# First chunk of a block-sparse attention with an expert MLP: exponentials in the gate's buffers, one head's ahead of the copies of the transposes

## The chip, the cores and the metric

The kernel runs on one core of a Trainium2 chip. The metric is the device time of one execution in microseconds (us). The engines are PE (matrix multiply), DVE (vector), ACT (scalar), POOL and SP; each takes its own instructions in the order in which the program wrote them, and they meet through semaphores. Transfers are issued from SP, ACT and POOL.

## What is computed

The attention is block sparse with 24 blocks of 32 positions. A query block sees itself and its neighbours, the first and last block, and three sampled blocks; the first and last query block see all. The attention's output goes through an MLP with the gate `h * sigmoid(1.702 h)`.

```python
scores = scale * np.matmul(q, k.transpose(0, 1, 3, 2))      # q, k, v: 4 x 8 heads x 768 x 64
scores = np.where(mask, scores, -1e9)
attn = np.exp(scores - scores.max(-1)); attn /= attn.sum(-1) + 1e-9
x = (attn @ v).transpose(0, 2, 1, 3).reshape(3072, 512)
h = x @ w_in                                                 # 512 x 2048
out = (h / (1 + np.exp(-1.702 * h))) @ w_out                 # 2048 x 512
```

## The kernel before

**Units and chunks.** A unit is 64 query rows (two blocks) of one batch, all eight heads; 48 units make six chunks of 512 tokens. The MLP works on one chunk at a time, in 16 steps over the hidden size, while the attention of the next chunk is spread between its matmuls (`tick`, `plan`). Only the attention of the first chunk has nothing to lie beside: `first` (L658) does items 0 to 8 (eight units of chunk 0 and one of chunk 1) before the first matmul of the MLP. All nine are sparse units.

**A round.** `first` is software pipelined. Its loop (L671) is called a round here, and round n works on three units:

- `scores` of unit n (L244): 32 small matmuls on PE into two banks (L260), one for each head of a pair. `least` (L278) adds the mask and takes the row minimum on DVE (L283, four instructions, two for each head), into `nm`. `exps` (L286) is four exponentials on ACT (L290), two for each head, which also sum the rows.
- `transposes` of unit n-1 (L296): eight on PE (L306), then two copies out of the banks on ACT into `pt` (L310), then the factors 1/sum on DVE (L360, L361). `values` of unit n-1 (L315): 64 small matmuls on PE (L331) that read `pt`; `normalise` (L365) scales their result into `x` on DVE (L373).
- `turn` of unit n-2 (L379): two transposes on PE (L384), a copy on ACT (`xhi`, L391), a subtraction on DVE (`xlo`, L392).

`self.early` is true in `first` alone. There `scores` hands back two steps, the minima of both heads and then the exponentials of both; `first` runs the second behind the copies of the transposes (L681). So ACT's round is: copy of `xhi`, two copies `pt`, four exponentials.

**Weights.** Between these steps `weights` (L398) converts the MLP's weights, read as pairs of 32-bit words of 64-bit floats: a load from ACT's queue into `raw` (L414, three buffers), an absolute value on ACT (L422), integer steps on DVE (L446, L452, L456), a copy on ACT (L459), a subtraction on DVE (L427). For the second matrix the result is saved to DRAM from ACT's queue (`ws`, L433), and `a` has three buffers, so that a later L422 waits until such a save has landed. From round 2 on, four steps of it run in each round: two between the minima and `turn` (L677), so that L422 stands on ACT ahead of `xhi`, and two at the end of the round (L686), with L456, L459 and the next load.

**Loads.** `loads` (L220) fetches keys and values for a pair of units into rings of two, from SP's and POOL's queues, once the pair before in the same slot has gone through its scores (keys) or its values.

**Buffers.** `ex` has four buffers of 384 columns (L289): the exponentials of unit n go over those of unit n-1, which the transposes have read by then. `ghi` and `glo` (L510, L518) are the split output of the gate, two buffers each of 512 columns; the MLP uses them from its first step on, and nothing before.

Of the kernel before, what the change touches and what calls it, by code (L numbers as in the profile page):

```python
# [9 lines left out]
F32 = mybir.dt.float32  # L10
F32R = mybir.dt.float32r
# [7 lines left out]
P = 128  # L19
# [12 lines left out]
CT = CU * UT  # L32
# [11 lines left out]
class Kernel:  # L44
# [57 lines left out]
    def indices(self):  # L102
# [7 lines left out]
        def take(shape):  # L110
            n = 1
            for k in shape:
# [8 lines left out]

        vblk = take([NB])
        first, second = slice(1, NB - 2, 2), slice(2, NB - 1, 2)
        nc.gpsimd.iota(vblk[3 * BLK:P, first], pattern=[[2, NU]], base=0, channel_multiplier=0,
                       allow_small_or_imprecise_dtypes=True)
# [20 lines left out]
        for i in range(NR):  # L146
            for cols, rows in ((first, slice(BLK * i, BLK * (i + 1))), (second, slice(BLK * (i + 1), BLK * (i + 2)))):
                nc.vector.tensor_copy(out=vblk[rows, cols], in_=sbw[rows, cols, i])
# [95 lines left out]
    def scores(self, g):  # L244
        nc, un, sparse = self.nc, g["unit"], self.sparse(g)
        r = g["k"]["n"] % RING
        g["k"]["scores"] -= 1
        if g["first"]:
            un["rs"] = self.small.tile([P, 2, NPAIR], F32, name="rs")
            un["nm"] = self.small.tile([P, 2, NPAIR], F32, name="nm")  # L250
        sps = self.psum("s", g["n"])
        if sparse:
            bi, n = un["b"] % 2, 2 * P
            kg = self.kg[r][:, :, bi].rearrange("p n (a s) -> p n a s", a=NPAIR)
            for i in range(2):
                for a in range(2):
                    for j in range(2):
                        for h in range(2):
                            pair, rows, c = 2 * i + a, slice(D * h, D * (h + 1)), 2 * a + j
                            nc.tensor.matmul(  # L260
                                sps[h][BLK * c:BLK * (c + 1), n * i:n * (i + 1)].rearrange("p (n s) -> p n s", s=BLK),
                                self.qt[r][rows, bi, UT * pair + BLK * j:UT * pair + BLK * (j + 1)],
                                kg[rows, 4 * j:4 * j + 8, pair], start=True, stop=True, tile_position=(D * h, BLK * c))
            parts = [(i, 0) for i in range(2)]
            bias = self.bias[:, un["u"]].rearrange("p (n o) -> p n o", o=1).broadcast_to([P, 8, BLK])
        else:
            kt = self.kg[r].rearrange("p n b c -> p (n b c)").rearrange("p (a s) -> p a s", a=NPAIR)
            i, half, n = g["i"], g["half"], S // 2
            for a in range(2):
                for h in range(2):  # L270
                    pair, rows = 2 * i + a, slice(D * h, D * (h + 1))
                    nc.tensor.matmul(sps[h][UT * a:UT * (a + 1), 0:n], self.qt[r][rows, 0, UT * pair:UT * (pair + 1)],  # L272
                                     kt[rows, pair, n * half:n * (half + 1)], start=True, stop=True, tile_position=(D * h, UT * a))
            parts = [(i, half)]
            bias = self.zero.broadcast_to([P, n])
        g["ex"] = {}

        def least(h):  # L278
            for k, (i, half) in enumerate(parts):
                at = sps[h][:, n * k:n * (k + 1)]  # L280
                if sparse:
                    at = at.rearrange("p (n s) -> p n s", s=BLK)
                nc.vector.tensor_tensor_reduce(out=at, in0=at, in1=bias, scale=-SCALE, scalar=3.0e38, op0=ALU.add, op1=ALU.min,  # L283
                                               accum_out=un["nm"][:, half, 2 * i + h:2 * i + h + 1])

        def exps(h):  # L286
            for k, (i, half) in enumerate(parts):
                c = 2 * i + h
                ex = g["ex"][h, k] = self.work.tile([P, 384], F32, name="ex", bufs=4)[:, 0:n]  # L289
                nc.scalar.activation(out=ex, in_=sps[h][:, n * k:n * (k + 1)], func=AF.Exp, bias=un["nm"][:, half, c:c + 1],  # L290
                                     scale=-1.0, accum_out=un["rs"][:, half, c:c + 1])

        return [lambda h=h: (least(h), exps(h)) for h in range(2)] if not self.early else [
            lambda: [least(h) for h in range(2)], lambda: [exps(h) for h in range(2)]]

    def transposes(self, g):  # L296

# [100 lines left out]
    def weights(self):  # L398
# [38 lines left out]
        fetch(1)  # L437
        yield
        first(0)
        for k, (f, i) in enumerate(todo):  # L440
            while i == 1 and f - WRING > self.downs - 1:
# [216 lines left out]
    def first(self):  # L658

        items = self.items[:CU + 1]  # L660
        assert items[CU]["unit"]["n"] == CU

        def finish(todo):
            while todo:
                todo.pop(0)()

        def weights(k):
            for _ in range(k):
                next(self.conv)

        for n, g in enumerate(items):  # L671
            if n == 1:
                next(self.conv)
            exps = self.scores(g)
            exps.pop(0)()
            if n > 1:
                weights(2)  # L677
                finish(self.turn(items[n - 2]))
            if n > 0:
                finish(self.transposes(items[n - 1]))  # L680
            finish(exps)  # L681
            if n > 0:
                finish(self.values(items[n - 1]))
            self.loads()
            if n > 1:
                weights(2)  # L686
        finish(self.turn(items[CU - 1]))
        self.loads()
# [64 lines left out]
```

## Time and profile before

| what | us |
|---|---|
| median of 3 runs (785.08 to 786.23) | 785.84 |
| the profiled execution, its own time | 782.75 |
| its span, first to last instruction | 781.1 |
| PE busy in the span | 738.6 (95%) |
| DVE busy | 412.8 (53%) |
| ACT busy | 383.5 (49%) |
| first matmul of the MLP starts at | 74.67 |

The profiled execution lies 3.09 us under the median of the runs. Times in rows are counted from the start of the span. A row of a timeline gives its start, its length, engine, line, operation, what it writes and reads, and in brackets how long the engine had been idle and what released it. A row that holds several instructions (x2) runs from the first's start to the last's end.

### The profile page before, as it was taken

To read this page: it belongs to the slowest core of one execution; us is meant where nothing else is said; L and a number is where in the kernel's file an instruction comes from. 1 tells how busy PE (TensorE), PEld (TensorE's weight loads), DVE (VectorE), ACT (ScalarE), POOL (GpSimd) and SP (SyncE) were. 2 spreads that over 40 slices of the span, in tenths; PEclk is the share of its full clock that TensorE was granted. 3 is DMA by queue.
4 is the path that set the end of the run, shared out by engine and by line. 5 is a ranking of instruction groups with operands and counts; after the bars stand their busy time and mean duration, and the time that the engine had idled before them with its cause. 6 is when DMAs were issued, how large, how long until landed. Compare 5 with 4: busy or idle time off the path is not lost.

```text
span 781.1 us, 19264 instructions
## 1 busy us (share of the span) xinstructions
PE 738.6 (95%) x7584; PEld 571.7 (73%) x7584; DVE 412.8 (53%) x1076; ACT 383.5 (49%) x950; POOL 57.1 (7%) x85
## 2 busy tenths in 40 slices
PE   2667999999999999999999999999999999999996
PEld 1445787767777777787877877877777777888884
DVE  3387779887644354445445544444554444443332
ACT  1567667666545444444444544444545454333332
POOL 5122001101000001000000000000000000000000
PEclk9699999999999999999999999999999999999998
DMA  8998887786644437664534465435574321041112
GB/s 267 281 367 296 251 254 256 251 259 222 206 162 153 117 114 219 173 177 129 161 117 145 142 175 156 137 115 163 161 229 153 93 98 42 28 108 40 55 41 55
DMA packets 61117, 128.22 MB, mean 164 GB/s; under 512 B 7569, under 2 KB 26514, under 8 KB 60514
## 3 DMA queue, kind: packets, MB, share of 16 engines
q1 hardware_dynamic: 46882, 80.50, 33.9%
q0 software_dynamic: 7232, 25.51, 10.1%
q10 hardware_dynamic: 6912, 20.97, 8.1%
q8 instruction: 60, 0.98, 0.5%
q14 instruction: 31, 0.25, 0.1%
HBM read 116.47 MB, written 10.49 MB: 163 GB/s over the span
## 4 chain that ended last, share of the span: by engine, by line
PE 78%; DMA 7%; DVE 7%; ACT 4%; issue 2%; SPq 1%; ACTq 0%; DVEq 0%
PE bank L491 11%; PE bank L541 10%; PE bank L542 10%; PE bank L537 10%; PE bank L493 10%; PE bank L492 10%; PE bank L260 5%; PE bank L306 4%; PE bank L331 4%; DMA ws<-a 3%; DMA kg<-in_kb_dram 2%; PE bank L339 2%; PE bank L272 2%; DMA raw<-in_moe_w_in_dram 2%; DVE a L452 1%
## 5 line engine op out<-in xcount | busy, mean ns | idle before, releaser
L491 PE MATMUL bank<-xhi,win 128*128 128x512 f32 x384 | 158.4, 412 | 1.2 <-ACT xhi L391 0.9
L290 ACT ACTIVATE ex<-bank,nm 128x256 f32<-128x256 f32 (+1 forms) x208 | 99.7, 492 | 115.4 <-DVE nm L283 113.6
L506 DVE SCALAR_TENSOR_TENSOR g<-g,bank 128x512 f32<-128x512 f32 x83 | 57.1, 687 | 183.8 <-ACT g L499 183.8
L541 PE MATMUL bank<-wout,ghi 128*128 128x512 f32 x384 | 154.1, 401 | 0.0
L542 PE MATMUL bank<-wout,ghi 128*128 128x512 f32 x384 | 151.7, 395 | 0.0
L493 PE MATMUL bank<-xhi,win 128*128 128x512 f32 x384 | 151.0, 393 | 0.0
L492 PE MATMUL bank<-xlo,win 128*128 128x512 f32 x384 | 150.0, 391 | 0.0
L499 ACT ACTIVATE g<-bank 128x512 f32<-128x512 f32 x96 | 57.5, 599 | 146.4 <-PE bank L493 146.1
L537 PE MATMUL bank<-wout,glo 128*128 128x512 f32 x384 | 107.7, 394 | 0.0
L480 DVE TENSOR_TENSOR wout<-wst,wout 128x512 fp32r<-128x512 f32 x80 | 55.4, 693 | 79.7 <-ACT wout L479 78.7
L511 ACT CAST ghi<-g 128x512 fp32r<-128x512 f32 x96 | 59.7, 622 | 54.6 <-DVE g L506 54.6
L491 PEld LDWEIGHTS bank<-xhi,win 128*128 128x128 f32 x384 | 72.1, 188 | 18.7 <-ACT xhi L391 1.1
L537 PEld LDWEIGHTS bank<-wout,glo 128*128 128x128 f32 x384 | 72.4, 189 | 17.3
L493 PEld LDWEIGHTS bank<-xhi,win 128*128 128x128 f32 x384 | 72.1, 188 | 16.3
L283 DVE CUSTOM_DVE_ANT_1 bank<-bank,bias 128x256 f32<-128x256 f32 x176 | 73.8, 440 | 19.3 <-PE bank L260 16.2
L542 PEld LDWEIGHTS bank<-wout,ghi 128*128 128x128 f32 x384 | 72.5, 189 | 15.6
L541 PEld LDWEIGHTS bank<-wout,ghi 128*128 128x128 f32 x384 | 72.2, 188 | 16.0
L492 PEld LDWEIGHTS bank<-xlo,win 128*128 128x128 f32 x384 | 72.3, 188 | 13.3 <-DVE xlo L392 0.3
L216 POOL DMA_INDIRECT vown<-in_v_dram,vidx x44 | 43.7, 994 | 496.9 <-PE bank L331 385.5
L260 PE MATMUL bank<-kg,qt 64*32 64x256 f32 x1408 | 55.8, 416 | 17.6 <-DMA vmid<-in_v_dram 10.5
L310 ACT COPY pt<-bank 128x512 f32<-128x512 f32 (+1 forms) x120 | 61.1, 563 | 19.4 <-PE bank L306 19.3
L331 PEld LDWEIGHTS bank<-vown,pt 128*32 128x32 f32 x1408 | 43.8, 113 | 31.8 <-ACT pt L310 16.0
(75 smaller groups left out, 821.8 us busy)
## 6 DMA issues: line engine op xcount, KB each, us to landing
wst<-ws SPq DMA_DIRECT2D x80, 256.0 KB, 2.7
kg<-in_kb_dram SPq DMA_DIRECT2D x136, 128.0 KB, 3.2
kg<-in_kb_dram SPq DMA_DIRECT2D x22, 384.0 KB, 4.9
raw<-in_moe_w_in_dram ACTq DMA_DIRECT2D x16, 512.0 KB, 9.7
raw<-in_moe_w_out_dram ACTq DMA_DIRECT2D x16, 512.0 KB, 4.5
kg<-in_kT_dram SPq DMA_DIRECT2D x4, 1536.0 KB
vown<-in_vd_dram SPq DMA_DIRECT2D x8, 768.0 KB, 6.0
qt<-in_q_dram SPq DMA_DIRECT2D x22, 256.0 KB, 4.9
```

The costliest lines, as they stand in the source:

```text
L260: nc.tensor.matmul(sps[h][BLK * c:BLK * (c + 1), n * i:n * (i + 1)].rearrange("p (n s) -> p n s", s=BLK), self.qt[r][rows, bi, UT * pair + ...
L283: nc.vector.tensor_tensor_reduce(out=at, in0=at, in1=bias, scale=-SCALE, scalar=3.0e38, op0=ALU.add, op1=ALU.min, accum_out=un["nm"][:, ha ...
L290: nc.scalar.activation(out=ex, in_=sps[h][:, n * k:n * (k + 1)], func=AF.Exp, bias=un["nm"][:, half, c:c + 1], scale=-1.0, accum_out=un["r ...
L310: copies.append(lambda pt=pt, ps=ps, m=m: nc.scalar.copy(out=pt[:, 0:m], in_=ps[:, 0:m]))
L331: nc.tensor.matmul(av[BLK * c:BLK * (c + 1), 0, 2 * i + h], g["pt"][h][:, 2 * i + k, BLK * c:BLK * (c + 1)], src[:, at:at + D], start=(k = ...
L491: nc.tensor.matmul(h, wih[:, k], hi[:, k], start=(k == 0), stop=False)
L492: nc.tensor.matmul(h, wih[:, k], lo[:, k], start=False, stop=False)
L493: nc.tensor.matmul(h, wil[:, k], hi[:, k], start=False, stop=(k == NCT - 1))
L511: self.nc.scalar.copy(out=ghi, in_=self.g[m][0])
L537: nc.tensor.matmul(o[n], glo[:, tk[n]], woh, start=False, stop=last)
L541: nc.tensor.matmul(o[n], ghi[:, tk[n]], woh, start=(f == 0), stop=False)
L542: nc.tensor.matmul(o[n], ghi[:, tk[n]], wol, start=False, stop=False)
```

## The change

In `first` the exponentials of a unit no longer go into four `ex` buffers. Those of one head (two instructions) go into one `ghi` buffer, those of the other into one `glo` buffer; with two buffers each, unit n does not write what unit n-1's transposes read. `scores` hands back three steps in place of two, and `first` runs the exponentials of the first head before the copies of the transposes of the unit before, those of the second head where all four stood. Rounds 1 to 8 change so; in round 0 no transposes precede. The later chunks keep their steps and their `ex` buffers.

```diff
--- before.py
+++ after.py
@@ -283,15 +283,20 @@
                 nc.vector.tensor_tensor_reduce(out=at, in0=at, in1=bias, scale=-SCALE, scalar=3.0e38, op0=ALU.add, op1=ALU.min,
                                                accum_out=un["nm"][:, half, 2 * i + h:2 * i + h + 1])
 
+        early = self.early
+
         def exps(h):
+            if early:
+
+                both = self.work.tile([P, CT], F32R, name=("ghi", "glo")[h]).bitcast(F32)
             for k, (i, half) in enumerate(parts):
                 c = 2 * i + h
-                ex = g["ex"][h, k] = self.work.tile([P, 384], F32, name="ex", bufs=4)[:, 0:n]
+                ex = g["ex"][h, k] = both[:, n * k:n * (k + 1)] if early else self.work.tile([P, 384], F32, name="ex", bufs=4)[:, 0:n]
                 nc.scalar.activation(out=ex, in_=sps[h][:, n * k:n * (k + 1)], func=AF.Exp, bias=un["nm"][:, half, c:c + 1],
                                      scale=-1.0, accum_out=un["rs"][:, half, c:c + 1])
 
         return [lambda h=h: (least(h), exps(h)) for h in range(2)] if not self.early else [
-            lambda: [least(h) for h in range(2)], lambda: [exps(h) for h in range(2)]]
+            lambda: [least(h) for h in range(2)], lambda: exps(0), lambda: exps(1)]
 
     def transposes(self, g):
 
@@ -676,6 +681,7 @@
             if n > 1:
                 weights(2)
                 finish(self.turn(items[n - 2]))
+            exps.pop(0)()
             if n > 0:
                 finish(self.transposes(items[n - 1]))
             finish(exps)
```

The instructions are the same on every engine; on PE, DVE, SP and POOL their order is the same too. On ACT the order changes. The first place is round 3, where ACT stands between the copy of `xhi` of unit 1 and the weights' copy L459. Before:

```order
L422 ACTIVATE a<-raw 128x512
L391 CAST xhi_120<-bank_91 128x4x64
L310 COPY pt<-bank_88 128x512
L310 COPY pt<-bank_92 128x512
L290 ACTIVATE ex,rs<-bank_89,nm 128x256 x2
L290 ACTIVATE ex,rs<-bank_90,nm 128x256 x2
L459 CAST win_102<-a 128x512
L414 DMA raw<-in_moe_w_out_dram 128x1024
```

And with the change (its lines are five further down from L296 on):

```order
L427 ACTIVATE a<-raw 128x512
L396 CAST xhi_120<-bank_91 128x4x64
L295 ACTIVATE ghi,rs<-bank_89,nm 128x256 x2
L315 COPY pt<-bank_88 128x512
L315 COPY pt<-bank_92 128x512
L295 ACTIVATE glo,rs<-bank_90,nm 128x256 x2
L464 CAST win_102<-a 128x512
L419 DMA raw<-in_moe_w_out_dram 128x1024
```

Two exponentials have moved ahead of the two copies `pt`, and nothing else has moved. The second place is round 6 on ACT, from the weights' copy at the end of round 5 to the weights' copy at its own end. Before:

```order
L459 CAST win_103<-a 128x512
L414 DMA raw<-in_moe_w_out_dram 128x1024
L422 ACTIVATE a<-raw 128x512
L391 CAST xhi_120<-bank_87 128x4x64
L310 COPY pt<-bank_88 128x512
L310 COPY pt<-bank_92 128x512
L290 ACTIVATE ex,rs<-bank_85,nm 128x256 x2
L290 ACTIVATE ex,rs<-bank_86,nm 128x256 x2
L459 CAST wout_118<-a 128x512
```

With the change:

```order
L464 CAST win_103<-a 128x512
L419 DMA raw<-in_moe_w_out_dram 128x1024
L427 ACTIVATE a<-raw 128x512
L396 CAST xhi_120<-bank_87 128x4x64
L295 ACTIVATE ghi,rs<-bank_85,nm 128x256 x2
L315 COPY pt<-bank_88 128x512
L315 COPY pt<-bank_92 128x512
L295 ACTIVATE glo,rs<-bank_86,nm 128x256 x2
L464 CAST wout_118<-a 128x512
```

Here too the absolute value L422 (now L427) and `xhi` stay ahead of all of it, and the two copies `pt` are now the fifth and sixth step behind the load.

## Rows read from the trace of the kernel before

**Rows 1.** Busy time in stretches: us, PE, PEld, DVE, ACT, POOL (instructions), clock, DMA, GB/s

```profile
37.60:47.60 10.00, 7.90 (x212) 5.82 (x212) 9.59 (x32) 7.92 (x26) 3.36 (x6) 0.93 1.03 377
74.60:180.00 105.40, 102.97 (x1126) 78.86 (x1130) 88.34 (x207) 73.17 (x168) 7.01 (x6) 1.00 0.80 256
180.00:781.00 601.00, 593.30 (x5586) 464.72 (x5574) 280.86 (x711) 272.66 (x672) 24.80 (x26) 1.00 0.43 131
```

**Rows 2.** The chain that ended last, up to 75 us: start, us, what

```profile
19.26 12.87 DMA raw<-in_moe_w_in_dram
...
33.08 0.50 ACT pt L310
33.62 2.00 PE bank L331 x64
35.61 2.00 PE bank L260 x32
37.61 0.41 DVE bank L283
...
47.56 0.34 ACT wout L459
47.94 9.68 DMA ws<-a
...
63.57 10.28 DMA kg<-in_kb_dram
```

**Rows 3.** Waits from 10 to 75 us: total us, times, longest

```profile
PE bank L331 <- ACT pt L310: 12.8, 7, 4.3
...
ACT pt L310 <- PE bank L306: 0.5, 1, 0.5
```

**Rows 4.** Timeline of ACT: start, us, what, count, [idle before <- releaser]

```profile
39.07 1.07 ACT L310 COPY pt<-bank 128x512 f32<-128x512 f32 x2 [0.54 <-PE bank L306]
40.03 0.49 ACT L290 ACTIVATE ex<-bank,nm 128x256 f32<-128x256 f32 x1
...
40.94 0.49 ACT L290 ACTIVATE ex<-bank,nm 128x256 f32<-128x256 f32 x1
...
57.71 0.69 ACT L422 ACTIVATE a<-raw 128x512 f32<-128x512 f32 x1 [2.85 <-DMA ws<-a]
...
74.24 0.37 ACT L391 CAST xhi<-bank 128x256 fp32r<-128x256 f32 x1 [0.57 <-DMA kg<-in_kb_dram]
```

**Rows 5.** Timeline of DVE: the normalisations of rounds 3, 4, 7 and 8

```profile
41.39 0.42 DVE L373 TENSOR_TENSOR x<-bank,ri 128x256 f32<-128x256 f32 x1
...
46.50 0.42 DVE L373 TENSOR_TENSOR x<-bank,ri 128x256 f32<-128x256 f32 x1
...
66.92 0.42 DVE L373 TENSOR_TENSOR x<-bank,ri 128x256 f32<-128x256 f32 x1
...
71.99 0.42 DVE L373 TENSOR_TENSOR x<-bank,ri 128x256 f32<-128x256 f32 x1
```

**Rows 6.** Timeline of PE: value matmuls, last of rounds 3, 4, 7, first of 6, 8

```profile
40.85 0.22 PE L331 MATMUL bank<-vown,pt 128*32 128x64 f32 x1
...
45.59 0.22 PE L331 MATMUL bank<-vown,pt 128*32 128x64 f32 x1
...
59.20 0.24 PE L331 MATMUL bank<-vown,pt 128*32 128x64 f32 x1 [2.46 <-ACT pt L310]
...
65.89 0.22 PE L331 MATMUL bank<-vmid,pt 128*32 128x64 f32 x1
...
70.50 0.24 PE L331 MATMUL bank<-vown,pt 128*32 128x64 f32 x1 [1.79 <-ACT pt L310]
...
71.65 0.22 PE L331 MATMUL bank<-vown,pt 128*32 128x64 f32 x1
```

**Rows 7.** Busy time in two stretches of PE's value and score matmuls, as rows 1

```profile
59.20:63.00 3.80, 3.80 (x97) 2.29 (x98) 1.54 (x4) 2.89 (x10) 1.43 (x2) 0.55 0.26 95
64.75:67.23 2.48, 2.42 (x96) 1.69 (x96) 2.34 (x8) 2.27 (x9) 1.04 (x2) 1.00 0.98 358
```

## The prediction

> **What bounds the kernel now.** I read first the busy time by stretches. From 180 us on PE is busy for 593.30 of 601.00 us, and from 74.60 to 180 for 102.97 of 105.40 [rows 1]: there the change touches nothing but the moment at which these stretches begin. Ahead of 74.6 PE waits, and the change lies there whole. In a good stretch of it, rounds 3 and 4, DVE works 9.59 of 10.00 us and PE only 7.90 [rows 1]. Then the chain of waits: in round 2 it goes from the copy `pt` on ACT to the value matmuls, the score matmuls of the next unit and the minima on DVE, without a gap; later it stays on DVE until the weights' copy at 47.56 and goes on through a save `ws` that takes 9.68 us to land; near the end it goes through a load of keys of 10.28 us [rows 2]. So rounds are of two kinds. Some are released by a landing, on ACT, and go through `pt` and PE; others are filled by DVE. Last, the waits: PE waited for `pt` seven times, 12.8 us in all; ACT waited for the transposes once, 0.54 us [rows 3, 4]. The reader is to see that `pt` is what PE waits for, and that the change puts work ahead of it.
>
> **What it removes and adds.** Nothing: the same instructions, the same sizes. The exponentials go to other buffers of the same memory, and no row shows another price for that; I take zero, between a gain of nothing (they never waited for those buffers: the copies `pt` before them had already waited for the transposes) and a loss of nothing.
>
> **What it moves.** Two exponentials now stand ahead of the two copies `pt`. The first of four started at 40.03 and the third at 40.94 [rows 4], so `pt` comes 0.91 us later wherever ACT does not wait. ACT ends its round when it did before, as the other two exponentials come 0.91 us later than the first of four did, and their sum is the same. No DMA is moved past anything: the loads and saves on ACT's queue stand behind all four in both orders, and those on SP and POOL keep their place, but wait for PE.
>
> The ScalarE page gives another price. The Trainium skill, "ScalarE: Activation LUTs", section "What ACT_TABLE_LOAD costs", puts an activation with a bias from memory at 280 ns plus 0.833 ns for each element, less 93 ns back to back: 400 ns here, so by it two would cost an estimated 0.80 us. The rows have 0.91, with the read of the row sum in it, and the sum below goes by the rows; by the page it would come to 1.8 us in place of 2.4.
>
> **Round by round.** Round 1: what ACT loses is covered by the weight load of round 2, which lands at 19.26 + 12.87 = 32.13 [rows 2] and for which ACT waits in either order; cost 0. Without that cover it would cost 0.91.
>
> Round 2 is released by that landing; ACT issued the load behind the exponentials of round 0, ahead of all moved work. From `pt` on the chain has no gap [rows 2]: values, scores, minima come 0.91 us later. **+0.91.**
>
> Round 3: ACT waited 0.54 us for the transposes before `pt` [rows 4]; the moved exponentials fill that, so `pt` is 0.91 - 0.54 = 0.37 us later. The last value matmul ended at 40.85 + 0.22 = 41.07 [rows 6], and DVE came to the normalisation at 41.39 [rows 5]: 0.32 us are covered. **+0.05.**
>
> Round 4: `pt` is 0.91 us later; values ended at 45.81 [rows 6], DVE came at 46.50 [rows 5]; 0.69 us are covered. **+0.22.**
>
> Round 5: everything in it comes later, but ACT then stands 2.85 us idle until 57.71 for the save issued at 47.94 [rows 2, 4]. **+0**, and the landing itself moves with its issue, by the 1.18 us so far. Without this cover it would be 0.91.
>
> Round 6 is released by that landing, and PE waits 2.46 us for `pt` [rows 6]. Values, scores and the loads of keys that are issued behind the scores at 63.57 [rows 2] come later by all of it. **+0.91.**
>
> Round 7: values ended at 65.89 + 0.22 = 66.11 [rows 6], DVE came at 66.92 [rows 5]; 0.81 us are covered. **+0.10.**
>
> Round 8: 71.65 + 0.22 = 71.87 [rows 6] against 71.99 [rows 5]; 0.12 us are covered. **+0.79.**
>
> The end: ACT stood 0.57 us idle before the last `xhi`, until a load of keys had landed [rows 4]. That landing moves by the 2.09 us up to round 6, and ACT's own way by 0.91 + 0.05 + 0.22 + 0.91 + 0.10 + 0.79 = 2.98 us, of which 0.57 were idle time: 2.41 us. The later one counts, **2.4 us**, and the first matmul of the MLP goes from 74.67 to about 77.1.
>
> Behind it I pass the 2.4 us on whole. The bounds are 0 (the next stretch makes it up) and 2.4. I take 2.4 because PE is busy for 102.97 of 105.40 us there [rows 1], so there is no room to make it up. The profiled execution took 782.75 us, so it would take 785.15; it lies 3.09 us under the median of the runs, 785.84, to which I add the same: **788.2 us**. A measurement of this kernel can tell 0.2%, 1.6 us, from no change.
>
> **Rival 1: the landings stay.** If the save that lands at 57.62 and what comes after is set by the traffic already queued and not by its issue, then what rounds 2 to 4 lose is swallowed in ACT's 2.85 us of idle time [rows 4]. Left are 0.91 + 0.10 + 0.79 - 0.57 = 1.23 us: 787.1 us, within 0.2%. For it speaks that a save of 9.68 us [rows 2] mostly queues. Against it speaks that most of what it queues behind is itself issued after the scores and values of rounds 3 and 4, and so moves along. The Trainium skill ("Trainium Kernel Development and Optimization", section "Key Constraints") says that the queues of SP, ACT and POOL share the same 16 DMA engines and interleave, which is what this rival needs; the rows agree as far as one save can show it. Chance 0.28.
>
> **Rival 2: faster.** Its place is ACT's wait for the transposes. Where ACT would wait there by more than 0.91 us, the two exponentials are free: `pt` comes no later, and the weights' copy, the next load and the next absolute value come earlier. The point from which it decides is thus a wait of 0.91 us ahead of `pt`. Such waits grow where PE runs slowly ahead of the transposes. The trace has one, of 0.54 us [rows 3]; three like it, filled and passed on whole with no loss elsewhere, give 1.62 us: 784.2 us. Against it: in the other rounds the transposes were done before ACT came to `pt`, and rounds 3 and 4 are DVE's [rows 1], to which an earlier ACT gives nothing. Chance 0.14.
>
> **Rival 3: PE's clock.** PE's wait for `pt` in round 6 was 2.46 us, and the granted clock fell: the values and scores after it took 3.80 us at a mean of 0.55, where in round 7 they took 2.48 us at 1.00 (full is 2.4 GHz, the other level 1.2) [rows 6, 7]. The wait in round 8 was 1.79 us, and I expect 2.70, longer than the one after which it fell. If it falls there, 1.32 us more are lost ahead of the end: 789.5 us; if it falls in round 4 also, 790.8. Against it: round 7 before it keeps PE busy. The Trainium skill, "TensorE: Matmul & The Clock Gate", section "HAM oscillation — how this bites in real kernels", describes short bursts of matmuls between waits that each start slow again; by that rule this rival is what one should expect of a longer wait, and the two stretches of rows 7 agree that such a wait cost 1.32 us. Chance 0.20.
>
> **How the numbers follow.** The forecast has 0.38, the rivals 0.28, 0.14 and 0.20. The forecast and rival 3 are slower by over 0.2% except for 0.01 (0.57 in all, and 0.01 from the upper edge of rival 1: 0.58). Rival 1 lies within 0.2% for 0.27; with 0.01 of the forecast and 0.01 of rival 2 that is 0.29. Rival 2 beyond 0.2% has 0.13. The range holds the forecast, rival 1 and the first case of rival 3: from 785.6, just under no change, since DVE's and ACT's idle time may cover more than I counted, to 790.6. Outside lie rival 2 and the far end of rival 3.
>
> **What would show it.** Right: the first matmul of the MLP at 76 to 78 us; PE's wait for `pt` over 12.8 us in all, by some 4 to 6; the normalisations of rounds 3, 4, 7 and 8 waiting for the values; the save of round 4 issued about 1.2 us later and landing later. Wrong: a first matmul at 74.7 or earlier, a longer idle time of ACT ahead of `pt` in the trace before than the one I found, or a gain behind 80 us that makes up what is lost.

## The result, and the profile after the change

The changed kernel took **788.82 us** (median of 20 runs, 786.60 to 790.69) beside 785.07 us for the kernel before in the same runs (median of 20): ratio **1.0054**, 95% interval 1.0043 to 1.0064. That is 4.2 us more (785.07 x 0.0054; 3.4 to 5.0; the two medians alone differ by 3.75). The forecast was 788.2 us, 2.4 us more. So the sign and the range hold, and the loss is nearly twice the one summed up. A loss in us is worked out below in this way throughout: the ratio less one, times the median of the kernel before that was measured beside it.

The profiled execution took 787.82 us with a span of 786.2 us. The first matmul of the MLP began at 79.38 us, where it was 74.67: 4.71 later, where the forecast had 2.4. From there on hardly anything differs, as these stretches show, which are laid some 5 us later than those of [rows 1] (view and columns as there):

```profile
79.40:185.00 105.60, 102.82 (x1122) 78.78 (x1126) 88.22 (x207) 72.58 (x166) 7.36 (x7) 1.00 0.81 256
185.00:786.00 601.00, 593.36 (x5590) 464.79 (x5578) 280.82 (x711) 273.00 (x672) 24.83 (x26) 1.00 0.43 131
```

PE is busy for 102.82 and 593.36 us; it was 102.97 of 105.40 and 593.30 [rows 1]. The spans differ by 5.1 us (786.2 and 781.1), so all but some 0.4 us of the loss lies in the first chunk, and it is passed on. The waits of the kernel after, 10 to 80 us (us in total, times, longest), answer to [rows 3]:

```profile
PE bank L336 <- ACT pt L315: 18.2, 7, 3.5
...
DVE x L378 <- PE bank L336: 9.6, 8, 3.1
```

PE waited 18.2 us for `pt`, where it was 12.8. DVE now waits for the value matmuls in all eight rounds, 0.34 us at the least. In the kernel before it was behind in four of them [rows 5], and the forecast had used that as a cover. What holds the first chunk is now one closed loop, as the chain of waits shows (start us, us, what), where [rows 2] went through a save and a load of keys:

```profile
47.63 1.02 ACT ghi L295 x4
48.65 0.97 ACT pt L315 x2
49.66 0.88 PE bank L336 x48
50.54 1.14 PE bank L260 x32
51.68 0.37 PE bank L389 x2
52.05 1.73 PE bank L311 x8
53.77 0.41 DVE bank L283
...
55.18 0.65 ACT ghi L295 x3
55.83 0.49 ACT pt L315
56.36 1.99 PE bank L336 x64
```

Exponentials and `pt` on ACT, then values, scores, turn and transposes on PE, the minima on DVE, exponentials again. In rounds 6 and 8 it goes from the transposes straight to ACT, and into round 4 and at the end through the normalisation and the weights' copy. No landing stands in it from 33.4 us to the MLP.

One thing in it no row of the kernel before had shown. The timeline of the kernel after, in round 3:

```profile
37.69 1.52 PE L260 MATMUL bank<-kg,qt 64*32 64x256 f32 x32
...
37.83 0.99 POOL L216 DMA_INDIRECT vown<-in_v_dram,vidx  x1 [16.05 <-PE bank L336]
...
39.13 0.44 PE L389 MATMUL bank<-ident,x 128*128 128x128 f32 x2
...
39.13 0.98 POOL L216 DMA_INDIRECT vown<-in_v_dram,vidx  x1 [0.30 <-issue]
...
39.41 0.60 PE L311 MATMUL bank<-ident,ghi 128*128 128x128 f32 x4
...
39.84 0.60 PE L311 MATMUL bank<-ident,glo 128*128 128x128 f32 x4
40.95 0.43 DVE L283 CUSTOM_DVE_ANT_1 bank<-bank,bias 128x256 f32<-128x256 f32 x1 [1.75 <-PE bank L311]
40.99 0.34 SPq L187 DMA_DIRECT2D qt<-in_q_dram  x1
41.04 0.37 ACT L396 CAST xhi<-bank 128x256 fp32r<-128x256 f32 x1 [0.93 <-PE bank L311]
...
42.01 0.47 ACT L295 ACTIVATE ghi<-bank,nm 128x256 f32<-128x256 f32 x1 [0.59 <-DVE nm L283]
...
42.92 1.07 ACT L315 COPY pt<-bank 128x512 f32<-128x512 f32 x2
```

The scores ended at 39.2 (37.69 + 1.52). DVE's minima wait for nothing but them, and began at 40.95, 1.75 us later; SP's load of `qt` and ACT's `xhi` began with them. By the trace's semaphore events PE's signals for the scores, the turn and the transposes came together, from 40.93 to 41.14, though by the rows these were done at 39.21, 39.57 and 40.44. (The profile models the ends of matmuls, so it does not show whether the signals alone were late or the end of the work too.) The same happens in rounds 5 and 7 and in no other round from the second on: there the minima begin 2.08 and 2.18 us behind the scores' end. In the kernel before, the minima of those rounds began 0.09 to 0.11 us behind it. I call these **late signals** below; the experiments first took them for a product of the change.

### The profile page after: what moved, and what is told of

It reads as the page before. It is cut to its first block, busy times and chain, and to the rows that moved or that the text cites. A ratio compares the mean times of both kernels' runs of the same rounds, so it can differ in the third digit from the quotient of the medians.

```text
span 786.2 us, 19250 instructions
## 1 busy us (share of the span) xinstructions
PE 736.4 (94%) x7584; PEld 571.2 (73%) x7584; DVE 412.3 (52%) x1076; ACT 383.6 (49%) x950; POOL 57.0 (7%) x85
## 4 chain that ended last, share of the span: by engine, by line
PE 80%; DVE 6%; ACT 5%; DMA 5%; issue 2%; SPq 0%; POOL 0%; ACTq 0%; POOLq 0%; DVEq 0%
PE bank L496 11%; PE bank L546 10%; PE bank L547 10%; PE bank L542 10%; PE bank L498 10%; PE bank L497 10%; PE bank L311 5%; PE bank L336 5%; PE bank L260 5%; DMA ws<-a 2%; PE bank L344 2%; DMA raw<-in_moe_w_in_dram 2%; PE bank L272 2%; DMA kg<-in_kb_dram 1%; ACT ex L295 1%
## 5 line engine op out<-in xcount | busy, mean ns | idle before, releaser
L295 ACT ACTIVATE ex<-bank,nm 128x256 f32<-128x256 f32 (+1 forms) x172 | 82.9, 491 | 115.2 <-DVE nm L283 113.4
L260 PE MATMUL bank<-kg,qt 64*32 64x256 f32 x1408 | 54.2, 407 | 19.0 <-DMA kg<-in_kb_dram 14.0
L336 PE MATMUL bank<-vown,pt 128*32 128x64 f32 x1408 | 52.9, 229 | 19.5 <-ACT pt L315 18.2
```

The lines of the kernel that those rows point to most:

```text
L260: nc.tensor.matmul(sps[h][BLK * c:BLK * (c + 1), n * i:n * (i + 1)].rearrange("p (n s) -> p n s", s=BLK), self.qt[r][rows, bi, UT * pair + ...
L336: nc.tensor.matmul(av[BLK * c:BLK * (c + 1), 0, 2 * i + h], g["pt"][h][:, 2 * i + k, BLK * c:BLK * (c + 1)], src[:, at:at + D], start=(k = ...
```

## The experiments

Theory P is the forecast: what stands ahead of `pt` on ACT is paid on PE, round by round. Theory B: the new buffers cost something. Theory S: the change's order of instructions makes PE's signals late. Later came H: the signals are late by chip or by execution, whatever the order. The kernels ran in three groups, e1 to e4, e5 to e8 and e9 to e12, each group on a chip of its own, with the kernel before measured beside it. The table gives the ratio to the kernel before on that chip, the loss worked out from it, and of the one profiled execution the first matmul of the MLP and whether rounds 3, 5 and 7 had late signals.

| run | ratio, 95% interval | loss, us | first MLP matmul, us | late signals |
|---|---|---|---|---|
| e1 buffers alone | 0.9994 [0.9976, 1.0012] | -0.5 | 75.89 | none |
| e2 order alone | 1.0020 [1.0000, 1.0039] | 1.6 | 78.12 | none |
| e3 other head ahead | 1.0068 [1.0042, 1.0093] | 5.3 | 82.04 | none |
| e4 transposes swapped | 1.0022 [1.0005, 1.0039] | 1.7 | 79.30 | none |
| e5 change again | 1.0051 [1.0033, 1.0069] | 4.0 | 79.76 | all three |
| e6 swap in even rounds | 1.0053 [1.0033, 1.0072] | 4.2 | 81.16 | all three |
| e7 weights behind exps | 0.9966 [0.9948, 0.9984] | -2.7 | 73.27 | all three |
| e8 weights ahead of exps | 0.9988 [0.9973, 1.0003] | -0.9 | 74.42 | all three |
| e9 before, here | 1.0003 [0.9987, 1.0019] | 0.2 | 75.61 | all three |
| e10 change, here | 1.0047 [1.0030, 1.0064] | 3.7 | 80.38 | all three |
| e11 swapped, here | 1.0053 [1.0035, 1.0070] | 4.2 | 79.76 | all three |
| e12 order, here | 1.0057 [1.0037, 1.0077] | 4.5 | 79.24 | all three |

**e1: the buffers alone.** The change without its moved call, so that all four exponentials stand behind `pt` again:

```diff
-            exps.pop(0)()
             if n > 0:
                 finish(self.transposes(items[n - 1]))
```

> The exponentials go to ghi and glo as in the change, but all four stand behind the copies pt as in the kernel before. Theory P (what costs is the place of two exponentials ahead of pt): the time of the kernel before, within 0.2%, and a first matmul of the MLP at 73.5 to 75.5 us. Rival B (the other buffers cost something themselves): slower than before by 1 us or more. Rival S (PE's signals of a round's scores reach DVE late when the first head's transposes wait for nothing, as the trace of the change shows in rounds 3, 5 and 7): those transposes wait again here, so as theory P, and DVE's minima start within 0.3 us of the scores' end in every round.

Measured: no loss (-0.5 us, from -1.9 to 0.9). The other buffers cost nothing, and B falls.

**e2: the order alone.** The order of the change, with the four buffers `ex` of the kernel before:

```diff
...
-                ex = g["ex"][h, k] = both[:, n * k:n * (k + 1)] if early else self.work.tile([P, 384], F32, name="ex", bufs=4)[:, 0:n]
+                ex = g["ex"][h, k] = self.work.tile([P, 384], F32, name="ex", bufs=4)[:, 0:n]
```

> The order of the change with the four ex buffers of the kernel before, so that the two early exponentials also wait until the first head's transposes have read them. Theory P: slower than before by 2.4 us or a little more (3 us), with minima that start within 0.3 us of the scores' end. Rival S: the first head's transposes wait for nothing here either, so 3.5 to 5 us slower than before, with minima 1.7 to 2.1 us behind the scores' end in some rounds. Rival B: less than half of the change's loss, under 2 us.

Measured: 787.6 us, a loss of 1.6 us (0 to 3.1), and no late signals. P's sign, with less than its 2.4; S had foreseen late signals here.

**e3: the other head ahead.** The second head's exponentials go ahead of `pt` and the first head's behind, while PE still transposes the first head first:

```diff
-            lambda: [least(h) for h in range(2)], lambda: exps(0), lambda: exps(1)]
+            lambda: [least(h) for h in range(2)], lambda: exps(1), lambda: exps(0)]
```

> The change with the second head's exponentials ahead of pt and the first head's behind. DVE has the second head's minima 0.91 us later than the first's, so pt comes later still. Theory P: slower than the change by 0 to 1.5 us, 4 to 5.5 us over the kernel before. Rival S: the first head's transposes, which stand first on PE, wait for ACT again, so the late signals go: 1 to 2.5 us over the kernel before, faster than the change by 1 to 3 us although pt is later.

Measured: 791.24 us, a loss of 5.3 us (3.3 to 7.3), as P had it. Its profile shows the price that the forecast lacks: a wait of the exponentials for DVE's minima (waits of e3, 25 to 75 us), four times, 1.1 us at the longest; the kernel before has no such wait in that stretch.

```profile
ACT glo L295 <- DVE nm L283: 3.6, 4, 1.1
```

**e4: the transposes swapped.** The change, with the second head's transposes first on PE in the first chunk and their copies in the old order:

```diff
...
-        for h, bank in enumerate(self.psum("t", g["n"])):
+        for h, bank in list(enumerate(self.psum("t", g["n"])))[::-1 if self.early else 1]:
...
+        if self.early:
+            copies.reverse()
```

> The change, with the second head's transposes ahead of the first head's on PE in the first chunk; ACT's order stays that of the change. So the transposes that stand first on PE wait for ACT again and those behind them for nothing, and pt is as late as in the change. Theory P: the time of the change, within 0.5 us, 3.5 to 4.5 us over the kernel before. Rival S: no late signals, DVE's minima within 0.3 us of the scores' end in rounds 3, 5 and 7, and 1.5 to 2.5 us over the kernel before.

Measured: 787.52 us, a loss of 1.7 us (0.4 to 3.1), no late signals. S had foreseen this number, and by it the case reads: 1.7 us from `pt`, some 2.5 us from late signals that the change's order brings about. That reading did not last: the unaltered change had not been run on that chip.

**e5 and e6: the change again, and the swap in half of the rounds.** e5 is the change unaltered. e6 swaps the transposes in rounds 2, 4, 6 and 8 alone:

```diff
...
+        for h, bank in list(enumerate(self.psum("t", g["n"])))[::-1 if self.early and g["n"] % 2 else 1]:
...
+        if self.early and g["n"] % 2:
+            copies.reverse()
```

> The changed kernel once more, unaltered, on another chip and in another execution. Theory S (PE's signals of the scores are held back in every other round, a property of this instruction order): the three late starts of DVE's minima in rounds 3, 5 and 7 come again, 1.7 to 2.2 us behind the scores' end each, the first matmul of the MLP starts at 78 to 80 us, and the kernel stays 3.5 to 4.7 us behind the kernel before. A rival C (an accident of that one execution or that chip): no late starts, first matmul at 76 to 77.5 us, 1.5 to 2.5 us behind the kernel before.

> The change, with the second head's transposes ahead of the first head's on PE in the even rounds only (2, 4, 6, 8); ScalarE's order is that of the change. With the swap in all rounds the late signals were gone. If the cause lies in the order of the round that is late (S, local): rounds 3, 5 and 7 keep the change's order, so their minima still start 1.7 to 2.2 us late, and the kernel stays 3.5 to 4.7 us behind the kernel before. If it lies in what the rounds ahead leave behind (S, from the round ahead): the late signals go or turn up elsewhere, and the kernel is 1.5 to 2.5 us behind.

Measured: losses of 4.0 us (2.6 to 5.4) and 4.2 us (2.6 to 5.7), both with late signals in rounds 3, 5 and 7 (in e6 the minima begin 1.30, 2.17 and 2.17 us behind the scores' end). That is what S, in its local form, had said, but for the first of these numbers. But e7 and e8, on the same chip, have the old order, and they had late signals as well.

**e7 and e8: what else stands ahead of `pt`.** Both are the kernel before with the first of a round's two calls `weights(2)` moved: in e7 behind the exponentials, in e8 ahead of the exponentials and behind the copies of the transposes.

```diff
             if n > 1:
-                weights(2)
                 finish(self.turn(items[n - 2]))
             if n > 0:
                 finish(self.transposes(items[n - 1]))
+            if n > 1:
+                weights(2)
             finish(exps)
```

This is e8; in e7 the two lines with the plus stand behind `finish(exps)`.

> The kernel before, with the first two of a round's four conversion steps called behind the exponentials of the round, not ahead of the turn. ScalarE then has neither the conversion's copy nor its absolute value (0.62 and 0.68 us, with their waits for DVE and for a weight's landing) between a round's scores and its copies of the transposes. Theory P (what stands ahead of the copies on ScalarE is paid on PE round by round): the copies come some 0.5 to 1.3 us earlier in the rounds that wait for them, the first matmul of the MLP starts at 70 to 73.5 us instead of 74.7, and the kernel is 1 to 4 us faster than the kernel before (781.5 to 784.5). Rival W (the conversion itself sets the end of the stage, since the MLP needs the weights): the copies come earlier, but the conversions come later, the first matmul stays at 74 to 76 us or its successors wait for weights, and the kernel is within 1 us of the kernel before or slower.

> The kernel before, with the same two conversion steps called behind the copies of the transposes and ahead of the round's exponentials. The copies come as early as with the steps behind the exponentials, but the exponentials, which the next round's transposes wait for, come after the conversion's work, as in the kernel before. Theory P: the copies are what PE waits for and the exponentials have slack until the next round, so it gains the same 1 to 4 us as the version with the steps behind the exponentials, within 1 us of it. Rival W: as there, within 1 us of the kernel before or slower.

Measured: e7 gains 2.7 us (1.3 to 4.1; the medians are 782.84 and 784.73), and **beats both kernels**: on this chip the change lost 4.0. e8 gains 0.9 us (-0.2 to 2.1), which is unclear; the gain within 1 us of e7's that P expected of it did not come, though the two intervals overlap. What P had left out shows in e8's waits (10 to 75 us): PE waits for `pt` for only 7.5 us, but three times for the exponentials that now stand behind the weights' work, 4.7 us in all (in e9 once, 2.1 us). In e7 PE's waits for `pt` fell, and ACT now waits for PE (waits of e7, 10 to 75 us):

```profile
PE bank L331 <- ACT pt L310: 9.4, 6, 3.9
...
ACT xhi L391 <- PE bank L384: 5.5, 2, 2.9
```

9.4 us instead of 14.6 in e9, the kernel before with late signals, as e7 has them, and 12.8 in [rows 3]: the converse of the change, and P in the other direction. Not all of it came through. At the second round's values e7 is 5.04 us ahead of the kernel before on the third chip (e9), and at the MLP 2.34 (73.27 against 75.61). The chain of e7 then goes through the weights' own way, a save and the load behind it:

```profile
50.59 7.68 DMA ws<-a
58.29 0.13 ACT a L422
58.46 8.83 DMA raw<-in_moe_w_in_dram
```

That is the rival W of these two, in part.

**e9 to e12: four kernels on one chip.** The kernel before, the change, the version of e4 and that of e2, all unaltered, each with a profile, to tell S from H.

> The kernel before, unaltered, with a profile of its own on the chip on which the next three are run. So far the first chip's four kernels had no late signals, and the second chip's four kernels had them in rounds 3, 5 and 7, all ending 3.07 to 3.13 us behind the last signal of the values, whatever their order. Theory H (late signals belong to the chip or to the execution, not to the change's order): the four kernels of this call agree, all with them or all without, this one too; with them its first matmul of the MLP starts later than 74.7 us, at 75.5 to 78. Theory S (they belong to the change's order on PE): this kernel has none, and its first matmul starts at 74 to 76 us. Its time against itself is 1.000 in both.

> The changed kernel on the same chip. Theory S: late signals in rounds 3, 5 and 7, first matmul at 78.5 to 80 us, 3.5 to 4.7 us behind the kernel before, and some 2.5 us behind the version with swapped transposes. Theory H: if the chip shows none, first matmul at 77 to 78.5 us and 1.5 to 2.7 us behind the kernel before, level with the swapped version within 1 us; if the chip shows them, it shows them in the other three kernels as well.

> The version with the second head's transposes ahead of the first head's on PE, on the same chip. Theory S: no late signals here, 1.5 to 2.5 us behind the kernel before and about 2.5 us ahead of the change. Theory H: it stands to the change within 1 us, with late signals or without as the change has them.

> The order of the change on ScalarE with the four old buffers of the exponentials, on the same chip. Theory S: no late signals, 1 to 2.5 us behind the kernel before and 2 to 3 us ahead of the change. Theory H: level with the change within 1 us, with late signals or without as the change has them.

Measured: all four have late signals, the kernel before too. **S falls, and H stands**: in each of the three groups the four kernels agree, whatever their order (none, all, all). In all eight profiles with late signals, and in that of the changed kernel, the first of them came 3.03 to 3.13 us behind the last signal of the value matmuls in rounds 3, 5 and 7, but for one round of e7 with 1.66. On this chip the change costs 3.7 us (2.4 to 5.0), the swapped version 4.2 (2.7 to 5.5) and the order alone 4.5 (2.9 to 6.0): one price within the intervals, for one order on ACT. On the first chip the last two cost 1.7 and 1.6.

The kernel before took 785.62 us (median) on the chip without late signals, and 784.73 and 784.6 us on the two with them: it hardly feels them. Why they are dear to the change all the same is seen on ACT. The timeline of ACT in the kernel before on this chip (e9), rounds 3, 5 and 7:

```profile
39.08 0.37 ACT L391 CAST xhi<-bank 128x256 fp32r<-128x256 f32 x1 [0.87 <-PE bank L306]
39.34 1.08 ACT L310 COPY pt<-bank 128x512 f32<-128x512 f32 x2
...
51.00 0.35 ACT L391 CAST xhi<-bank 128x256 fp32r<-128x256 f32 x1
51.25 1.08 ACT L310 COPY pt<-bank 128x512 f32<-128x512 f32 x2
...
64.82 0.37 ACT L391 CAST xhi<-bank 128x256 fp32r<-128x256 f32 x1 [0.48 <-PE bank L306]
65.09 1.08 ACT L310 COPY pt<-bank 128x512 f32<-128x512 f32 x2
```

And that of the change on the same chip (e10):

```profile
39.83 0.37 ACT L396 CAST xhi<-bank 128x256 fp32r<-128x256 f32 x1 [0.87 <-PE bank L389]
40.79 0.47 ACT L295 ACTIVATE ghi<-bank,nm 128x256 f32<-128x256 f32 x1 [0.59 <-DVE nm L283]
...
41.71 1.07 ACT L315 COPY pt<-bank 128x512 f32<-128x512 f32 x2
...
53.37 0.36 ACT L396 CAST xhi<-bank 128x256 fp32r<-128x256 f32 x1
54.30 0.47 ACT L295 ACTIVATE ghi<-bank,nm 128x256 f32<-128x256 f32 x1 [0.57 <-DVE nm L283]
...
55.21 1.07 ACT L315 COPY pt<-bank 128x512 f32<-128x512 f32 x2
...
69.03 0.37 ACT L396 CAST xhi<-bank 128x256 fp32r<-128x256 f32 x1 [0.48 <-PE bank L311]
69.99 0.47 ACT L295 ACTIVATE ghi<-bank,nm 128x256 f32<-128x256 f32 x1 [0.59 <-DVE nm L283]
...
70.91 1.07 ACT L315 COPY pt<-bank 128x512 f32<-128x512 f32 x2
```

In the kernel before, `pt` begins 0.25 to 0.27 us behind the start of `xhi`, since the transposes' signals have come with all the others. In the change it begins 1.84 to 1.88 us behind it: the exponentials ahead of it first wait 0.57 to 0.59 us for the minima, which themselves began late, and then take their 0.92. So a round with late signals pays some 1.6 us, not 0.91. In e2, the same order without late signals, the wait is there once, and short (timeline of ACT in e2, round 3):

```profile
38.57 0.37 ACT L393 CAST xhi<-bank 128x256 fp32r<-128x256 f32 x1 [0.21 <-PE bank L386]
39.13 0.47 ACT L292 ACTIVATE ex<-bank,nm 128x256 f32<-128x256 f32 x1 [0.19 <-DVE nm L283]
...
40.05 1.07 ACT L312 COPY pt<-bank 128x512 f32<-128x512 f32 x2
```

There the signals of the scores come 0.6 us ahead of the turn's, the minima are nearly done when `xhi` is, and `pt` begins 1.48 us behind it, of which 0.19 us is that wait.

## Why the prediction was right in sign and short in size

The best comparison is e9 with e10: the same chip, both with late signals, one execution each. The forecast closed its rounds at DVE's normalisation, where DVE's lateness covers PE's. When the normalisation of each round began, us:

| round | e9, before | e10, change | later by | grown by | forecast |
|---|---|---|---|---|---|
| 1 | 24.57 | 25.12 | 0.55 | 0.55 | 0 |
| 2 | 35.96 | 36.71 | 0.75 | 0.20 | 0.91 |
| 3 | 42.79 | 44.18 | 1.39 | 0.64 | 0.05 |
| 4 | 47.89 | 50.17 | 2.28 | 0.89 | 0.22 |
| 5 | 54.19 | 57.55 | 3.36 | 1.08 | 0 |
| 6 | 61.69 | 65.88 | 4.19 | 0.83 | 0.91 |
| 7 | 68.53 | 72.97 | 4.44 | 0.25 | 0.10 |
| 8 | 73.61 | 78.38 | 4.77 | 0.33 | 0.79 |
| MLP | 75.61 | 80.38 | 4.77 | 0 | -0.57 |

The forecast's sum was 2.41. Rounds 3, 5 and 7 grew by 1.97 us in all where it had 0.15, rounds 4 and 8 by 1.22 where it had 1.01, rounds 1, 2 and 6 by 1.58 where it had 1.82, and the end gave nothing back where it had 0.57.

- **What it removes and adds: zero.** Right; e1 shows it.
- **Two exponentials ahead of `pt`, 0.91 us.** Right where a landing releases the round, in rounds 2 and 6. ACT of e9, then of e10:

```profile
32.41 0.66 ACT L422 ACTIVATE a<-raw 128x512 f32<-128x512 f32 x1 [1.35 <-DMA raw<-in_moe_w_in_dram]
...
58.13 0.67 ACT L422 ACTIVATE a<-raw 128x512 f32<-128x512 f32 x1 [2.26 <-DMA ws<-a]
```

```profile
32.79 0.67 ACT L427 ACTIVATE a<-raw 128x512 f32<-128x512 f32 x1 [2.98 <-DMA raw<-in_moe_w_in_dram]
...
61.41 0.68 ACT L427 ACTIVATE a<-raw 128x512 f32<-128x512 f32 x1 [2.18 <-DMA ws<-a]
```

From these starts to the first value matmul (33.88 and 59.60 in e9, 35.16 and 63.78 in e10) it is 1.47 us in e9 and 2.37 in e10, in both rounds: 0.90 us more. Round 2 shows less in the table because its value matmuls took 1.99 us in e9 and 1.47 in e10.

- **The same 0.91 us in rounds 3, 5 and 7.** Here the sum failed. The step left out that these exponentials wait for DVE's minima. In the kernel before the copies `pt` stood between, so that no row showed a wait there. This is a wait that the change adds, and it is paid ahead of `pt`: 0.59, 0.57 and 0.59 us in e10. With it the price in these rounds is the 1.6 us found above. PE shows it too: from one normalisation to the end of the next values it took 2.02, 1.33 and 1.61 us longer in e10, and 1.60, 1.67 and 1.62 without the difference in the length of these value matmuls themselves.
- **The covers of rounds 3, 5 and 7.** DVE's lateness at the normalisation [rows 5] was there in e9, and larger than the forecast had it: 1.43, 0.30 and 1.43 us behind the values' end, as late signals hold DVE up in the kernel before as well. In e10 it is 0.05 to 0.07. So it covered most of the price in rounds 3 and 7, and little in round 5. The other two covers failed. ACT's wait of 0.54 us for the transposes in round 3 [rows 4] was not there: in e9 `pt` follows `xhi` at once. And ACT's idle time for the save, which was to make round 5 free, gave 0.08 us: 2.26 us in e9 and 2.18 in e10.
- **The save's landing moves with its issue.** Not by the same amount. By its semaphore events this save landed 9.68 us behind its issue in the first profile of the kernel before, 7.72 in that of the change, and 8.71, 9.70, 8.49 and 7.13 in e9 to e12. So what ACT's idle time covers goes by the execution. In e12 ACT did not wait for the save at all. In the first pair of profiles the cover worked: the change issued the save at 52.07 instead of 47.94, it landed 2.17 us later, and ACT came to it behind the landing; the 2.85 us of idle time were used up.
- **Rounds 4 and 8: 0.22 and 0.79.** They grew by 0.89 and 0.33. DVE's lateness covered 0.61 us of round 4 (forecast 0.69), but ACT had some 0.6 us of small waits there on top of the 0.91.
- **The end, -0.57.** It gave nothing: no load of keys holds ACT there in e9, and the MLP begins 2.00 us behind the last normalisation in both.
- **The size as a whole.** The forecast was summed from a trace without late signals, and where there are none it stands, as far as was measured: 2.4 us lies in both intervals measured on the chip without them, e2's 0 to 3.1 and e4's 0.4 to 3.1. The profile of the result has them. That the sum was still over half of the 4.2 us is in part luck: in e9 and e10 a price that was too small met covers by DVE that were larger than assumed.
- **Passed on whole behind the first chunk.** Right to some 0.4 us: see the stretches above.
- **Rival 1, the landings stay.** In part. They do not stay, but in the first pair of profiles the save's landing moved by 2.17 us where its issue moved by 4.13, and ACT's idle time swallowed 2.85 us, as this rival has it; yet the MLP began 4.71 us later, as the rounds ahead had lost more than the rival assumed (the first value matmul of round 5 came 4.8 us later). In e10 the landing moved by more than its issue (3.28 and 2.29 us). The Trainium skill ("Trainium Kernel Development and Optimization", section "Key Constraints") says that the transfers of the three queues run on the same 16 DMA engines and interleave; no run here tells whether that moves this landing.
- **Rival 2, faster.** No: ACT's longest wait for the transposes ahead of `pt` is the 0.54 us of [rows 4]; in e9, with late signals, there is none from round 2 on, for there `xhi`, which stands ahead of the exponentials, waits for the signals.
- **Rival 3, PE's clock.** Not in the first pair of profiles. The granted clock was at its lower level (1.2 GHz) for 20.5 us of the first 80 in both (before: two times 6.8 and two times 3.4; after: 10.2 and three times 3.4). PE's wait in the last round, 1.47 us, was shorter than the 2.70 that this rival needed; the clock fell in round 7 instead, toward the end of a wait of 3.54 us, and no longer in round 6. In e10 it was at that level for 23.9 us beside 20.5 in e9, so a part of that pair's difference can be the clock's.
- **What would show it.** PE's wait for `pt` rose by 5.4 us, inside the 4 to 6 given, and the normalisations of rounds 3, 4, 7 and 8 wait for the values. The first matmul at 79.38 lies outside 76 to 78, and the save's issue moved by 4.1 us instead of 1.2.

How much late signals add is an estimate: the same two kernels lose 1.6 and 1.7 us on the chip without them, and 4.5 and 4.2 us on a chip with them, so some 2.5 to 2.9 us. The intervals overlap a little (e2's ends at 3.1 us, where e12's begins at 2.9), and two chips may differ in more than this, so it is not shown as a size. That a wait for the minima, three to five times and at most 0.6 or 0.7 us long, stands ahead of `pt` in every kernel with this order and late signals is shown (after, e5, e6, e10, e11, e12); without late signals e2 and e4 have one each, of 0.2 and 0.4 us.

## What to carry to other kernels

Ask of every instruction that is moved ahead of a copy what it waits for itself: the price is its length and its own wait, and that wait may be hidden in the trace of before by the very copy that it now precedes. A cover read from one trace (an engine that was late anyway, a landing waited for) has its size from that execution: the same save left ACT idle for 2.85, 2.26 and 2.18 us in the kernel before, e9 and e10, and for 0.6 and 0 us in e11 and e12. The engine order that gained here was the opposite one: e7 took work that waits for landings away from ahead of the copy on which PE waits. And an odd timing in one profile is put down to the change only after the old kernel was profiled on the same chip.

## What the runs showed of the hardware that was not expected

From round 2 on late signals come only in rounds 3, 5 and 7, the rounds in which POOL issues two gathers of `vown` (0.98 us each) while PE computes the next scores. In round 3 of the kernel after they run from 37.83 to 40.11 (rows above), and PE's signals come from 40.93 on. In the kernel before, the same two gathers ran, and the signals passed between them (timeline, round 3):

```profile
35.69 0.98 POOL L216 DMA_INDIRECT vown<-in_v_dram,vidx  x1 [14.49 <-PE bank L331]
...
36.97 0.97 POOL L216 DMA_INDIRECT vown<-in_v_dram,vidx  x1 [0.30 <-issue]
...
37.59 0.43 DVE L283 CUSTOM_DVE_ANT_1 bank<-bank,bias 128x256 f32<-128x256 f32 x1 [0.53 <-PE bank L260]
37.63 0.34 SPq L187 DMA_DIRECT2D qt<-in_q_dram  x1
```

The second gather began at 36.97, and DVE and SP saw the scores' signal at 37.6, in the middle of it. The late ones come 3.03 to 3.13 us behind the values' last signal, in all late rounds but one, and in the kernel after the two gathers start within 0.12 us of that signal and are over 2.3 to 2.4 us behind it.

There is a fourth such place, ahead of round 1, where two gathers run beside the first unit's scores and end at 16.72 to 16.75 us in all 14 profiles. In the nine with late signals the scores' signal comes at 17.20 to 17.29, though these scores end anywhere from 16.09 to 17.16. In the five without it comes 0.04 to 0.05 us behind the scores' end, in the kernel before at 16.25, while the second gather still runs. So the same nine profiles stand apart before the change can act. That the signals wait until the gathers are over would fit these times, but it is argued and not shown, and round 7 of e7 speaks against it in its plain form: there a PE signal came at 57.98, between the two gathers, and another at 58.72, during the second.

The fetching of instructions does not explain it: packets of that queue lie near two of the three late rounds of the kernel after, and near the third there is none between 63.2 and 73.4 us. Whether the chip, the loading of the program or the execution decides it stays open: the three groups used three chips, one each, the chips of the first two profiles are not on record, and each run has one profile. Whether the gathers hold the signals was not tried; a version that issues them elsewhere would tell.
